# Four stores for the running products, an earlier fetch of block 1's decays, and five whole steps in a planned one-core kernel

## The chip, the core and the metric

The kernel runs on one core of one Trainium2 chip. The metric is the device time of one execution in microseconds (us), taken as the median of several runs. Engines are named as the profile names them: PE (TensorE; PEld is its weight load), DVE (VectorE), ACT (ScalarE), POOL (GpSimd) and SP (SyncE, whose queue SPq issues nearly all transfers here).

## The reference

Three layers follow one another. The first is a chunked linear recurrence over 4 batches, 8 heads and 768 positions; the other two are feed-forward layers on its output, each 256 to 2048 to 256.

```python
# recurrence, one chunk at a time (a is the decay, cum its running log sum)
L = np.exp(cum[:, :, :, None] - cum[:, :, None, :]) * causal
y_intra = np.einsum('bhij,bhjd->bhid', CB * L, xc)
y_inter = np.einsum('bhin,bhnd->bhid', Cc, state) * np.exp(cum)[:, :, :, None]
state = decay_full * state + np.sum(Bx, axis=2)
# layer 1 and layer 2, x is 3072 x 256
g = np.maximum(h, 0.0) + np.log1p(np.exp(-np.abs(h)))          # h = x @ w_in
g = np.where(h >= 1, h, np.where(h <= -1, 0.0, (h + 1) ** 2 / 4))
out = g @ w_out
```

## The kernel before

The sequence is cut into six blocks of 128 positions (`NC`), each for four batches, so there are 24 units `u` (block `u // 4`, batch `u % 4`). Block 0 makes its decay matrix on PE and ACT. Blocks 1 to 5 work on half blocks of 64: the clipped decays are stored once to a DRAM buffer `clip_z` (job `store`), then for each pair of units `rows` fetches them back, spread over 64 partitions (L1080, two transfers for a pair, one for each half), and `decay` turns them into the decay matrix by one scan on DVE (L1110). The running products of the decays are made by job `runs` (one scan on DVE at L1054), stored to the DRAM buffer `clip_p` by `store_runs` (L1059, one transfer for each of the blocks 1 to 5) and fetched for a block by `dec` (L1087), spread over the 16 state columns. `cd` (L1130, DVE) multiplies the unit's C by them, `carry` and `ready` use them for the state.

The two feed-forward layers are 192 steps `s`: a step takes one block's tokens and one of 16 slices of the hidden width (the first four steps take half a block's tokens and two slices). `up(s)` is the product with the input weights, `g(s)` the activation on ACT, `down(s)` the product with the output weights, accumulated in two PSUM banks of the block. To keep float32 accuracy, a number is split into a high and a low part (fp32r), and a product takes three matmuls (high by high, low by high, high by low; L1314 to L1316 for `up`, L1450 for `down`). The first `WHOLE` steps make their `down` otherwise: the activation is written in float32 straight into a `gh` buffer and the matmul runs on unsplit float32 operands (L1438). A step that isn't whole has two jobs more: `g_hi` (rounds the activation, L722, ACT or DVE) and `g_lo` (the remainder, L1424, DVE, or POOL for steps below 16), and its output weights must have been split (`w_hi` at L722, `split_w` at L955 on DVE or POOL). Until step 15, PE has two PSUM banks for `up`, so it can be two steps ahead of the activation. Weights arrive as 64-bit numbers and are made into float32 by `w0` to `w3` (L781 to L817) on ACT and DVE.

Nothing of the order is written by hand: `program` lists all jobs with an engine or a choice of engines, a cost, the jobs that they need and the buffers that they take, and `Jobs.order` simulates the engines in Python when the kernel is built and emits the jobs in the order in which that simulation started them. On each engine, SP's queue among them, instructions then run in this fixed order, so one that waits holds up all behind it. Constants steer the plan: `BIAS` is added to an engine's finish where there is a choice, `RATE` is the assumed rate of the transfers in bytes per ns, `RUSH` moves single jobs' due times (positive: sooner), `STAND_BY` lets a more urgent job go first, `CHUNK`, `SPACE` and `SHIFT` give the steps by which later blocks are due, `LAG_1` the due time of some `down` jobs. `BIAS_2` would apply to a `split_w` of the second layer on POOL; these have no such choice. In the first 26 us the emitter also puts fillers (bf16 matmuls on zeros, L1531) where the plan has PE idle.

Of the kernel before, what the change touches and what calls it, by code (L numbers as in the profile page):

```python
# [16 lines left out]
HALF = 64  # L17
# [10 lines left out]
class Jobs:  # L28
# [18 lines left out]
    def order(self, slots, begin):  # L47
# [33 lines left out]
        locked, shared = [], None  # L81
# [19 lines left out]
        for _ in range(len(jobs)):  # L101
# [25 lines left out]
            if engine == POOL:  # L127

                begun = start + 60
                for a, b in locked:  # L130
                    if a < begun + cost and b > begun:
                        begun = b
                shared = [name, begun, begun + cost]
                cost += begun - start
            elif engine == DVE and kind in LOCKED:
                if shared and start < shared[2] and start + cost > shared[1]:
                    if start <= shared[1]:
                        late = start + cost - shared[1]
                        shared[1] += late
                        shared[2] += late  # L140
# [11 lines left out]
            if engine == SP:  # L152
                pipe = max(pipe, end) + size / RATE
                end = pipe + BEHIND * (start < 5000.0 and size > 2e5)
            done = self.done[name] = end
# [84 lines left out]
def program():  # L240
# [34 lines left out]
    add("runs", DVE, 1500, needs=["clip", ("columns", 1)] + RUNS)  # L275
    for c in range(1, NC):
        add(("store_runs", c), SP, 600, needs=["runs"], size=16e3)
        add(("dec", c), SP, 400, needs=[("store_runs", i) for i in range(1, NC if c == 2 else 2)], takes=["dec"], size=262e3)
    for u in range(NU):
# [12 lines left out]
        else:  # L292
            if b % 2:
                add(("rows", u), SP, 1100, needs=["store"], takes=["lp"], size=524e3)
# [229 lines left out]
WHOLE = 8  # L524
# [19 lines left out]
BIAS = {DVE: 400, POOL: 500}  # L544
# [3 lines left out]
STAND_BY = 400  # L548
FAR = 10000.0
CHUNK = 9  # L550
BIAS_2 = 9000
RATE = 330.0
# [4 lines left out]
SHIFT = 2  # L557
LAG = 1500
LAG_1 = 9000
# [9 lines left out]
    ("decay", 2, 1): -8000, ("decay", 5): -16000, ("load_w", 1, "i", 2): -16000, ("w3", 0, "o", 4): 8000,  # L569
# [8 lines left out]
def tile_kernel(ctx: ExitStack, tc: tile.TileContext, a0, al, bc, ub, w_in, w_out, w2_in, w2_out, out):  # L578
# [132 lines left out]
    clip_z = dram.tile([NU, 2, H * HALF], F32, name="clip_z")  # L711
# [5 lines left out]
    clip_p = dram.tile([NC, H, NB * 2, HALF], F32, name="clip_p")  # L717
# [319 lines left out]
    def store(engine, *step):  # L1037
# [7 lines left out]
        else:  # L1045
            nc.sync.dma_start(clip_z.rearrange("u s (h i) -> (u s) h i", h=H), z_t)
# [9 lines left out]
    @job  # L1056
    def store_runs(engine, c):
        n = NB * 2
        nc.sync.dma_start(clip_p[c].rearrange("h r i -> r h i"), tiles["clip"][c * n:(c + 1) * n])  # L1059
# [16 lines left out]
    def rows(engine, u):  # L1076

        t = flat(buf(*got["rows", u][0])).rearrange("p (u f) -> p u f", u=2)
        for s in range(2):
            nc.sync.dma_start(  # L1080
                t[s * HALF:(s + 1) * HALF], clip_z[u - 1:u + 1, s].unsqueeze(0).to_broadcast([HALF, 2, H * HALF])
            )

    @job
    def dec(engine, c):
        src = clip_p[c].rearrange("h r i -> h (r i)")
# [498 lines left out]
```

## Time and profile before

| What | us |
|---|---|
| median of 3 runs | 557.3 (556.88 to 559.26) |
| the profiled execution, its own time | 557.88 |
| its span, first to last instruction | 556.2 |
| PE busy | 546.8 |
| DVE busy | 435.7 |
| ACT busy | 391.7 |
| POOL busy | 39.2 |

The span leaves out about 1.7 us ahead of the first and behind the last instruction. Busy time of PE counts fillers, and the ends of matmuls are modelled, so a busy PE is no proof of useful work. The granted clock of PE was 1.00 through the span.

### The profile page before, as it was taken

To read this page: it belongs to the slowest core of one execution; us is meant where nothing else is said; L and a number is where in the kernel's file an instruction comes from. 1 tells how busy PE (TensorE), PEld (TensorE's weight loads), DVE (VectorE), ACT (ScalarE), POOL (GpSimd) and SP (SyncE) were. 2 spreads that over 40 slices of the span, in tenths; PEclk is the share of its full clock that TensorE was granted. 3 is DMA by queue.
4 is the path that set the end of the run, shared out by engine and by line. 5 is a ranking of instruction groups with operands and counts; after the bars stand their busy time and mean duration, and the time that the engine had idled before them with its cause. 6 is when DMAs were issued, how large, how long until landed. Compare 5 with 4: busy or idle time off the path is not lost.

```text
span 556.2 us, 10449 instructions
## 1 busy us (share of the span) xinstructions
PE 546.8 (98%) x3994; PEld 442.3 (80%) x3994; DVE 435.7 (78%) x813; ACT 391.7 (70%) x720; POOL 39.2 (7%) x45
## 2 busy tenths in 40 slices
PE   9898999999999999999999999999999999999997
PEld 4765878878888888888888788888888888888885
DVE  6987999888865989876777898989886665876663
ACT  7968646645455666766566989786987875888773
POOL 3112220000000100001300000021310000000000
PEclk9999999999999999999999999999999999999999
DMA  8985467576242500276436314514100001100002
GB/s 280 392 220 178 138 194 210 165 235 183 93 165 75 180 1 1 96 258 205 143 113 214 128 59 152 171 56 130 62 1 0 1 1 38 39 0 1 1 1 76
DMA packets 34679, 64.73 MB, mean 116 GB/s; under 512 B 3684, under 2 KB 8164, under 8 KB 34628
## 3 DMA queue, kind: packets, MB, share of 16 engines
q1 hardware_dynamic: 34484, 63.93, 35.3%
q8 instruction: 31, 0.51, 0.4%
q14 instruction: 20, 0.16, 0.1%
q10 hardware_dynamic: 144, 0.13, 0.1%
HBM read 47.61 MB, written 16.43 MB: 115 GB/s over the span
## 4 chain that ended last, share of the span: by engine, by line
PE 87%; DMA 8%; DVE 2%; ACT 1%; SPq 1%; issue 1%; DVEq 0%; ACTq 0%
PE acc L1450 44%; PE h L1321 5%; PE h L1323 5%; PE h L1322 5%; PE z L1321 4%; PE z L1323 4%; PE z L1322 4%; PE h L1314 3%; PE h L1315 3%; PE h L1316 3%; DMA raw<-in_w_out_dram 2%; DMA ld<-clip_z 2%; DMA dec<-clip_p 2%; PE y L1223 1%; DMA st<-in_w_out_dram 1%; DMA u<-in_ub_dram 1%
## 5 line engine op out<-in xcount | busy, mean ns | idle before, releaser
L1424 DVE TENSOR_TENSOR gl<-g,gh 128x512 fp32r<-128x512 f32 x181 | 127.6, 709 | 55.1 <-PE acc L1450 31.0
L1450 PE MATMUL acc<-gh,woh 128*128 128x512 f32 x368 | 144.3, 392 | 0.0
L1450 PE MATMUL acc<-gh,wol 128*128 128x512 f32 x368 | 143.3, 389 | 0.0
L722 ACT CAST gh<-g 128x512 fp32r<-128x512 f32 x172 | 106.8, 621 | 26.4 <-PE acc L1450 14.2
L1450 PE MATMUL acc<-gl,woh 128*128 128x512 f32 x368 | 113.6, 389 | 0.0
L1450 PEld LDWEIGHTS acc<-gh,woh 128*128 128x128 f32 x368 | 69.1, 188 | 15.2 <-issue 0.5
L1450 PEld LDWEIGHTS acc<-gl,woh 128*128 128x128 f32 x368 | 69.1, 188 | 14.4
L1450 PEld LDWEIGHTS acc<-gh,wol 128*128 128x128 f32 x368 | 69.1, 188 | 14.1
L1409 ACT ACTIVATE g<-h 128x512 f32<-128x512 f32 x61 | 36.4, 597 | 51.7 <-PE h L1316 36.6
L1401 ACT ACTIVATE t<-t 128x512 f32<-128x512 f32 x96 | 60.9, 634 | 1.9
L1314 PE MATMUL h<-xh,wih 128*128 128x512 f32 (+1 forms) x114 | 46.0, 403 | 0.5 <-ACT wih L722 0.5
L1315 PE MATMUL h<-xh,wil 128*128 128x512 f32 (+1 forms) x114 | 42.9, 376 | 0.7 <-DVE wil L955 0.7
L1316 PE MATMUL h<-xl,wih 128*128 128x512 f32 (+1 forms) x114 | 42.9, 376 | 0.0
L1110 DVE TENSOR_TENSOR_SCAN ld<-ld,eye_t 128x512 f32<-128x512 f32 x20 | 25.1, 1289 | 4.0 <-DMA ld<-clip_z 2.7
L1394 ACT ACTIVATE t<-h 128x512 f32<-128x512 f32 x37 | 22.1, 598 | 7.8 <-PE h L1323 6.7
L1314 PEld LDWEIGHTS h<-xh,wih 128*128 128x128 f32 x114 | 21.4, 188 | 6.2 <-issue 1.1
L1413 DVE TENSOR_TENSOR g<-h,t 128x512 f32<-128x512 f32 x37 | 25.3, 685 | 1.1 <-ACT t L1401 0.3
L1394 ACT ACTIVATE t<-z 128x512 f32<-128x512 f32 x35 | 21.0, 599 | 7.1 <-DVE g L1413 3.9
L1315 PEld LDWEIGHTS h<-xh,wil 128*128 128x128 f32 x114 | 21.5, 188 | 5.6 <-DVE wil L955 1.0
L1413 DVE TENSOR_TENSOR g<-z,t 128x512 f32<-128x512 f32 x35 | 24.0, 686 | 1.5 <-ACT t L1401 0.5
L1316 PEld LDWEIGHTS h<-xl,wih 128*128 128x128 f32 x114 | 21.4, 188 | 4.0
L1409 ACT ACTIVATE g<-z 128x512 f32<-128x512 f32 x19 | 11.4, 598 | 17.4 <-PE z L1316 8.8
(320 smaller groups left out, 1008.0 us busy)
## 6 DMA issues: line engine op xcount, KB each, us to landing
st<-in_w_in_dram SPq DMA_DIRECT2D x15, 512.0 KB, 5.9
st<-in_w_out_dram SPq DMA_DIRECT2D x15, 512.0 KB, 6.7
u<-in_ub_dram SPq DMA_DIRECT2D x24, 256.0 KB, 6.2
ld<-clip_z SPq DMA_DIRECT2D x20, 256.0 KB, 6.0
bc<-in_bc_dram SPq DMA_DIRECT2D x12, 384.0 KB, 6.5
pre_i<-st_plain SPq DMA_DIRECT2D x15, 256.0 KB, 2.0
pre_s<-st_plain SPq DMA_DIRECT2D x14, 192.0 KB, 5.5
pre_o<-st_plain SPq DMA_DIRECT2D x10, 256.0 KB, 3.7
```

The costliest lines, as they stand in the source:

```text
L722: nc.scalar.copy(out, in_)
L1314: nc.tensor.matmul(o, wh, xh[c][:, k, t0:t0 + n], start=(k == 0), stop=False)
L1315: nc.tensor.matmul(o, wl, xh[c][:, k, t0:t0 + n], start=False, stop=False)
L1316: nc.tensor.matmul(o, wh, xl[c][:, k, t0:t0 + n], start=False, stop=(k == 1))
L1321: nc.tensor.matmul(bank, wh, bh, start=start, stop=False, skip_group_check=True)
L1322: nc.tensor.matmul(bank, wl, bh, start=False, stop=False, skip_group_check=True)
L1323: nc.tensor.matmul(bank, wh, bl, start=False, stop=True, skip_group_check=True)
L1401: nc.scalar.activation(out=t, in_=t, func=AF.Square, scale=0.5 / SAT, bias=0.5)
L1409: nc.scalar.activation(out=g, in_=ph, func=AF.Softplus)
L1413: nc.vector.tensor_tensor(out=g, in0=ph, in1=t, op=ALU.max)
L1424: engines[engine].tensor_tensor(out=mine("g_lo", s)[0], in0=mine("g", s)[0], in1=mine("g_hi", s)[0].bitcast(F32), op=ALU.subtract)
L1450: nc.tensor.matmul(acc_t(s, e), w, g[:, j * n:(j + 1) * n], start=(begins(e, j) and g is gh and i == 0), stop=(fc + j == NFC - 1 and g is ...
```

## The change

Five things are changed together.

1. `store_runs` is two jobs of two transfers each in place of five of one. Job 1 stores block 1 (one transfer for each half of a block), job 2 stores blocks 2 to 5. `dec(1)` needs job 1, all later `dec` need job 2. Before, `dec(1)` needed the first store, `dec(2)` all five, and later ones the first.
2. The DRAM buffers are laid out anew: `clip_z` by half first (a pair's `rows` transfer then reads one run of 4 KB where it read two of 2 KB), `clip_p` by head first. The host array `al` is transposed to match.
3. `WHOLE` is 5 in place of 8, so steps 5, 6 and 7 become split steps.
4. The planner's model: SP is given at most eight transfers in flight, `rows` and `dec` are charged more bytes, and the lock that POOL and DVE share is modelled more simply.
5. The planner's constants.

```diff
             if engine == POOL:
-                begun = start + 60
-                for a, b in locked:
-                    if a < begun + cost and b > begun:
-                        begun = b
-                shared = [name, begun, begun + cost]
+                begun = max([b for a, b in locked if a < start + 60 < b], default=start + 60)
+                shared = [name, begun, begun + cost, False]
...
+                flight += [end + 1500] * TRANSFERS.get(name if isinstance(name, str) else name[0], 1)
+                if len(flight) >= 8:
+                    clock[SP] = max(clock[SP], flight[-8])
...
+    for c in range(1, 3):
+        add(("store_runs", c), SP, 700, needs=["runs"], size=16e3 * (c * c))
     for c in range(1, NC):
-        add(("store_runs", c), SP, 600, needs=["runs"], size=16e3)
-        add(("dec", c), SP, 400, needs=[("store_runs", i) for i in range(1, NC if c == 2 else 2)], takes=["dec"], size=262e3)
+        add(("dec", c), SP, 400, needs=[("store_runs", min(c, 2))], takes=["dec"], size=262e3 * 1.5)
...
-                add(("rows", u), SP, 1100, needs=["store"], takes=["lp"], size=524e3)
+                add(("rows", u), SP, 1100, needs=["store"], takes=["lp"], size=524e3 * 1.6)
...
-WHOLE = 8
+WHOLE = 5
-BIAS = {DVE: 400, POOL: 500}
+BIAS = {DVE: 600, POOL: 1500}
-STAND_BY = 400
+STAND_BY = 300
-CHUNK = 9
-BIAS_2 = 9000
-RATE = 330.0
+CHUNK = 10
+BIAS_2 = 500
+RATE = 385.0
+TRANSFERS = {"rows": 2, "store_runs": 2, "split_w": 2, "put_w": 2, "put_s": 2, "get_s": 2}
-SHIFT = 2
+SHIFT = 1
-LAG_1 = 9000
+LAG_1 = 12000
 RUSH = {
-    ("decay", 2, 1): -8000, ("decay", 5): -16000, ("load_w", 1, "i", 2): -16000, ("w3", 0, "o", 4): 8000,
+    ("down", 31): -4000, ("sources", 9): -4000, ("w2", 0, "i", 5): 4000,
 }
...
-    clip_z = dram.tile([NU, 2, H * HALF], F32, name="clip_z")
+    clip_z = dram.tile([2, NU, H * HALF], F32, name="clip_z")
-    clip_p = dram.tile([NC, H, NB * 2, HALF], F32, name="clip_p")
+    clip_p = dram.tile([H, NU, 2, HALF], F32, name="clip_p")
...
     def store_runs(engine, c):
-        n = NB * 2
-        nc.sync.dma_start(clip_p[c].rearrange("h r i -> r h i"), tiles["clip"][c * n:(c + 1) * n])
+        a, b = ((NB, 2 * NB), (2 * NB, NU))[c - 1]
+        for s in range(2):
+            nc.sync.dma_start(clip_p[:, a:b, s].rearrange("h u i -> u h i"), tiles["clip"][s * NU + a:s * NU + b])
...
-                t[s * HALF:(s + 1) * HALF], clip_z[u - 1:u + 1, s].unsqueeze(0).to_broadcast([HALF, 2, H * HALF])
+                t[s * HALF:(s + 1) * HALF], clip_z[s, u - 1:u + 1].unsqueeze(0).to_broadcast([HALF, 2, H * HALF])
...
-        src = clip_p[c].rearrange("h r i -> h (r i)")
+        src = clip_p[:, c * NB:c * NB + NB].rearrange("h u s i -> h (u s i)")
```

## Rows read from the trace of the kernel before

**Rows 1.** The page: busy us of each engine, share of the span, instructions.

```profile
PE 546.8 (98%) x3994; PEld 442.3 (80%) x3994; DVE 435.7 (78%) x813; ACT 391.7 (70%) x720; POOL 39.2 (7%) x45
```

**Rows 2.** Waits of PE, whole span: us in total, times, longest.

```profile
PE acc L1438 <- ACT gh L1409: 2.1, 2, 1.5
...
PE h L1315 <- DVE wil L955: 0.7, 1, 0.7
PE h L1314 <- ACT wih L722: 0.5, 1, 0.5
PE z L1321 <- ACT h L1349: 0.2, 1, 0.2
```

**Rows 3.** Windows: stretch, busy us (instructions) of each engine, PE clock, DMA share, GB/s.

```profile
30.00:40.00 10.00, 10.00 (x39) 6.96 (x38) 9.66 (x17) 6.19 (x10) 0.00 (x0) 1.00 0.77 202
40.00:50.00 10.00, 8.27 (x27) 4.62 (x26) 5.30 (x13) 6.60 (x12) 0.00 (x0) 1.00 0.67 198
...
500.00:556.20 56.20, 52.12 (x230) 42.83 (x229) 33.16 (x51) 38.62 (x68) 0.00 (x0) 1.00 0.05 20
```

**Rows 4.** Timeline of PE, 19 to 80 us: start, us, instruction [idle before].

```profile
19.59 1.99 PE L1438 MATMUL acc<-gh,w 128*128 128x256 f32 x8 [1.51 <-ACT gh L1409]
...
35.00 0.80 PE L1314 MATMUL h<-xh,wih 128*128 128x512 f32 x1
...
38.11 0.80 PE L1314 MATMUL h<-xh,wih 128*128 128x512 f32 x1
...
43.72 1.98 PE L1438 MATMUL acc<-gh,w 128*128 128x512 f32 x4 [0.55 <-ACT gh L1409]
...
47.63 0.50 PE L1314 MATMUL h<-xh,wih 128*128 128x512 f32 x1 [0.53 <-ACT wih L722]
48.78 0.50 PE L1315 MATMUL h<-xh,wil 128*128 128x512 f32 x1 [0.66 <-DVE wil L955]
...
79.34 0.80 PE L1223 MATMUL y<-ld,u 64*32 64x64 f32 x60 [0.82 <-DVE ld L1166]
```

**Rows 5.** The chain in order of time, two split steps after another.

```profile
110.07 1.36 PE acc L1450 x6
112.79 1.36 PE acc L1450 x6
```

**Rows 6.** Timeline of DVE, 26 to 46 us.

```profile
26.61 1.68 DVE L817 SCALAR_TENSOR_TENSOR w<-st,w 128x512 uint32<-128x512 uint32 x1
...
40.04 0.68 DVE L955 TENSOR_TENSOR wol<-w,woh 128x512 fp32r<-128x512 f32 x1
45.42 0.90 DVE L1130 TENSOR_TENSOR u<-u,dec 128x128 f32<-128x128 f32 x4 [4.70 <-DMA dec<-clip_p]
```

**Rows 7.** Timeline of SP's queue, 23 to 35 us: start, us from first to last issue.

```profile
23.30 3.60 SPq L1080 DMA_DIRECT2D ld<-clip_z  x4
27.04 6.60 SPq L1059 DMA_DIRECT2D clip_p<-more  x5
34.25 0.41 SPq L769 DMA_DIRECT2D st<-in_w_in_dram  x1
```

**Rows 8.** The chain from 19 to 62 us: two transfers, issue to landing.

```profile
26.32 9.42 DMA ld<-clip_z
...
36.23 9.16 DMA dec<-clip_p
```

**Rows 9.** Waits of SP's queue, 20 to 50 us.

```profile
SPq L769 <- DVE w L817: 10.3, 2, 7.8
```

**Rows 10.** The page's groups: us busy, mean ns of one.

```profile
L1424 DVE TENSOR_TENSOR gl<-g,gh 128x512 fp32r<-128x512 f32 x181 | 127.6, 709 | 55.1 <-PE acc L1450 31.0
...
L722 ACT CAST gh<-g 128x512 fp32r<-128x512 f32 x172 | 106.8, 621 | 26.4 <-PE acc L1450 14.2
```

**Rows 11.** Timeline of POOL at 26 us: two products' low parts.

```profile
26.44 2.99 POOL L955 TENSOR_TENSOR wol<-w,woh 128x512 fp32r<-128x512 f32 x2 [10.89 <-ACT woh L722]
```

**Rows 12.** The page's transfers: KB each, median us from issue to landing.

```profile
pre_i<-st_plain SPq DMA_DIRECT2D x15, 256.0 KB, 2.0
```

More of the change, by code (lines that the diff above doesn't have):

```diff
@@ L80, in order @@
         held = {}
-        locked, shared = [], None
+        locked, shared, flight = [], None, []
         self.start, self.end, self.done = {}, {}, {}
@@ L136, in order @@
                 if shared and start < shared[2] and start + cost > shared[1]:
-                    if start <= shared[1]:
+                    if start <= shared[1] and not shared[3]:
                         late = start + cost - shared[1]
-                        shared[1] += late
-                        shared[2] += late
+                        shared[1:] = shared[1] + late, shared[2] + late, True
                         clock[POOL] = self.done[shared[0]] = shared[2]
@@ L1045, in store @@
         else:
-            nc.sync.dma_start(clip_z.rearrange("u s (h i) -> (u s) h i", h=H), z_t)
+            nc.sync.dma_start(clip_z.rearrange("s u (h i) -> (s u) h i", h=H), z_t)
     @job
@@ L1551 @@
     c6 = C.reshape(NB, H, NC, Q, N)
-    al = np.ascontiguousarray(a.reshape(NB, H, NC, 2, HALF).transpose(2, 0, 3, 1, 4)).reshape(NC * NB * 2, H * HALF)
+    al = np.ascontiguousarray(a.reshape(NB, H, NC, 2, HALF).transpose(3, 2, 0, 1, 4)).reshape(NC * NB * 2, H * HALF)
     a0 = np.ascontiguousarray(a6[:, :, 0]).reshape(NB * H, Q)
```

## The prediction

> **What bounds the kernel now.** I read the page first: PE is busy for 546.8 of 556.2 us, DVE for 435.7, the others for less [rows 1]. So the time is PE's work plus the few microseconds in which PE stood, and the next view is the list of PE's waits [rows 2]. Once PE has begun, it gives 4.3 us in six waits over the whole span; placed in the timeline, all but the 0.2 us of the wait for L1349 lie before 80 us [rows 2, 4]. The reader is to see that behind that point nothing is to be won but work taken off PE, and that a new order there can only lose. The tail of 4.1 us, where the last stretch has PE busy for 52.12 of 56.20 [rows 3], is the last copies and stores, which the change leaves alone.
>
> What is left ahead of 80 us: 1.51 us before 19.59 (the larger of the two waits at L1438), 0.55 before 43.72, 0.53 and 0.66 before 47.63 and 48.78, and 0.82 before 79.34 (block 2's products with its decay matrix) [rows 4]. To see why, I followed DVE back from the two waits at 48 us. DVE finished a split at 40.7 and then stood 4.70 us until block 1's running products landed (`cd`, L1130) [rows 6]; the weights of step 8, which PE wanted at 47.1, were queued behind it on DVE. The stretch from 40 to 50 us shows it from outside: DVE is busy for 5.30 of 10, PE for 8.27 [rows 3]. The running products were late because of SP's queue: four row transfers from 23.3, five stores from 27.0 to 33.6, weight loads from 34.25, and only then the fetch at 36.23, which took 9.16 us to land [rows 7, 8].
>
> **What the change takes and costs, part by part.** *Three steps less on float32.* A whole step runs six split matmuls and its float32 `down`: the periods at 35.00 and 38.11 are 3.11 us apart [rows 4]. A split step is twelve matmuls in two groups, 2.72 us (110.07 to 112.79) [rows 5]. Three steps give 3 x (3.11 - 2.72) = 1.17 us of PE work. This is the surest term, since PE is full from 19.6 to 43 us.
>
> *What these three steps ask for instead.* Each needs a rounding (0.62 us, ACT) and a remainder (0.71 us on DVE) [rows 10], or a remainder on POOL at 1.5 us, half of the 2.99 us that two like products took there [rows 11]: 3 x 0.71 = 2.1 us of DVE, and the low parts of two pieces of the output weights, which the old order made at leisure, are due some 10 us sooner. I cost this at nothing, because the 4.70 us hole in DVE's queue [rows 6] covers the 2.1 us if the decays come in time. If that cover is gone, up to 2.1 us land on PE. Making them on POOL has a price too: the L817 at 26.61 took 1.68 us while POOL was at its products from 26.44, where another product of that size takes DVE 0.68, so a POOL product can cost DVE about 1.0 us [rows 6, 11]. The higher bias against POOL should make that rarer and give DVE 0.7 us for each product moved back, so the two nearly cancel.
>
> *The decays fetched sooner.* Four transfers go out in place of five, and block 1's fetch waits for the first two of them, which are half a block's products each. With the stores no longer all ahead of it, the fetch can go out from about 27 to 32 instead of 36.23; an estimate from the same queue is that it lands 4 to 9 us sooner. DVE reached the wait at 40.7, so 4.70 us sooner is enough: the hole closes, and the 0.53 and 0.66 us at PE [rows 4] with it: 1.19 us. What is late next on that path is the weights themselves: SP had waited up to 7.8 us for a staging buffer that DVE's last weight operation frees (L769 behind L817) [rows 9], and that wait sits behind the same hole, so I expect it to shrink, not to take over.
>
> *The wait at 43.7.* PE stood 0.55 us for the activation of step 7, written late because ACT stood for a weight load in its queue [rows 4]. Step 7's `down` is split after the change, so it follows later and PE takes the next `up` first. I take all of the 0.55; the bounds are 0 and 0.55.
>
> *Rows by halves.* Each `rows` transfer reads runs of 4 KB, not two of 2 KB; one of them took 9.42 us [rows 8]. At best the scans of block 1 start some us sooner. They end on no PE wait here, so I cost it at nothing, with block 2's 0.82 us [rows 4] as the upper bound of what it can give.
>
> *The new constants and the model of SP.* They reorder everything. Behind 80 us PE stood 0.2 us, so a gain there is excluded but a loss isn't; in the first 20 us PE waits for ACT's first activation, and ACT's choice of work there may move either way by one operation, 0.6 us [rows 10]. I take zero, bounds -1.5 (the first wait at L1438 gone) and +2.6 (new waits as large as all those that the old order has from 40 to 80 us: 0.55 + 0.53 + 0.66 + 0.82 [rows 4]).
>
> *A rule weighed against the rows.* On the first two stores, the nearest row for a small transfer to DRAM is 2.0 us to landing (256 KB, later in an idle stretch), and the farthest 9.42 us, for the `rows` transfer that stood in the queue at the same time [rows 8, 12]. The Trainium skill, DMA: Bandwidth & Descriptors, "Anatomy of one DMA — SWDGE (gpsimd) path", puts the fixed cost at about 2.0 us and says that a semaphore wait happens on the issuing sequencer before dispatch; the idle row agrees with the figure, and no row here shows a store's landing under load; by its 2.0 us the fetch would go out about 2 us behind the first store and the sum would be the same 554.4. By the row of 9.42 us SP would stand up to 9 us with the weights behind it, and that is the slower rival below.
>
> **The sum.** On the profiled execution's own 557.88: 1.17 + 1.19 + 0.55 = 2.91, which gives 554.97. That execution lies 0.6 above the median of 557.3, so on the median it is 554.4.
>
> **The rivals.** *More than that.* With SP's queue modelled by what it can hold, the 0.82 us of block 2 and half of the first 1.51 us go as well: another 1.6 makes 552.8. For it speaks that both waits are for work that other engines could have done sooner; against, that the first of them waits for ACT's first activation, to which the change does nothing that the code shows.
>
> *The gain is spent on the new work.* The three split `down` steps need 2.1 us of DVE and two pieces of weights sooner, in the stretch from 30 to 45 us where DVE would now be full. Then a wait of 1 to 3 us for a low part takes the place of those removed: 555.4 to 557.4, inside 0.5% of before. For it: DVE is nearly full in the old order already (9.66 of 10 in the slice before the hole) [rows 3].
>
> *The change doesn't do what it says.* The fetch still lands behind 40 us, since the transfers ahead of it are the bound and not the stores; only the 1.17 us stay: 556.1.
>
> *Slower.* SP's queue is in order. If the fetch of block 1 stands for the landing of its stores while the stores queue behind a megabyte of rows, the landing takes up to 9.42 us [rows 8], and the weight loads behind it (from 34.25 in the old order [rows 7]) go out by as much later. PE needs these weights from 47.1, and waited 1.19 us for them already; with 7 us more it would end at 557.3 - 1.2 + 7 = 563.1. It turns the sign once the delay on PE is more than the 2.9 us gained, and passes 0.5% at 5.7 us. Against it: the rows go out 3.6 us ahead in the old order and most of their landing time is over when the stores end.
>
> **How the numbers follow.** The forecast of 554.4 has 45 in 100, with 553.4 to 555.6 as its own range; more gain 20, the gain spent on new work 20, no effect but the 1.17 us 5, slower 10. A measurement of this kernel tells about 0.5%, 2.8 us, from no change, so faster means below 554.5. Of the forecast's 45, a little over half fall below that, so with the 20 of more gain it is 46 in 100. Same is the rest of the forecast, the spent gain and the lone 1.17 us: 43. Slower is the last rival and the bad end of spent gain: 11. The range that holds 8 in 10 runs from 552.3, the lower end of more gain, to 557.4, the upper end of spent gain.
>
> **What would show each step.** Right: four L1059 issues, the first two ahead of the first L1087; the fetch landing before 40 us; no wait of L1130 for it over 1 us; L1438 at five steps, 9 us or less of PE; L1314 and L1315 without waits around 48 us; PE's waits between 20 and 80 us at about 0.8 us in all. Wrong: PE waiting at L1450 for `gl` or `wol` between 35 and 55 us (the gain was spent), SP standing at L1087 with L769 behind it (the slower rival), waits of PE behind 80 us (the new order), or a first wait at L1438 above 1.5 us. The prediction falls if PE's work has not become about 1.2 us shorter, or if new waits ahead of 80 us exceed 1 us in sum.

## The result and the profile after

The changed kernel takes 564.0 us (563.56 to 564.25, four runs) against 557.3 (556.88 to 559.26) beside it: ratio 1.0126, 95% interval 1.0109 to 1.0144. It is slower by 1.3%, some 7 us. A second set of runs of the same kernel gave 564.6 (561.87 to 565.86), ratio 1.0134 (1.0100 to 1.0168). The forecast of 554.4 and its range are both missed, on the side that had 11 in 100. The profiled execution took 563.56 with a span of 561.8.

The first line of the page answers to [rows 1]:

```profile
PE 549.1 (98%) x3998; PEld 445.1 (79%) x3998; DVE 441.8 (79%) x804; ACT 401.7 (71%) x738; POOL 36.7 (7%) x42
```

PE is no less the bound than before, and DVE and ACT do more. PE's waits over the whole span answer to [rows 2] (L1533 belongs to the fillers, L1483 lies at the very start):

```profile
PE acc L1440 <- ACT gh L1411: 3.0, 1, 3.0
PE h L1323 <- POOL xh_later L725: 1.6, 1, 1.6
PE h L1483 <- DVE idle L1481: 1.1, 1, 1.1
PE y L1225 <- DVE ld L1168: 1.0, 3, 0.5
PE h L1533 <- ACT ld L1114: 0.6, 1, 0.6
PE acc L1203 <- issue: 0.6, 1, 0.6
PE z L1323 <- DVE z L1366: 0.5, 2, 0.3
```

The code has grown by two lines, so L1440 is L1438 of before, L1225 is L1223, and so on. The two waits for split weights (L1314, L1315) and the second one at L1438 are gone, as forecast. But the first wait at the `down` has doubled from 1.51 to 3.0 us, and there is a new 1.6 at L1323, in the second layer. In the timeline of PE they stand here, beside [rows 4]:

```profile
20.49 3.78 PE L1440 MATMUL acc<-gh,w 128*128 128x256 f32 x8 [3.01 <-ACT gh L1411]
...
48.27 0.80 PE L1225 MATMUL y<-ld,u 64*32 64x64 f32 x60 [0.53 <-DVE ld L1168]
...
50.27 0.30 PE L1203 MATMUL acc<-u,bt 64*32 64x64 f32 x3 [0.56 <-issue]
...
72.87 0.63 PE L1225 MATMUL y<-ld,u 64*32 64x64 f32 x32 [0.24 <-DVE ld L1168]
...
399.67 0.47 PE L1323 MATMUL h<-eye_later,wih 128*128 128x512 f32 x1 [1.62 <-POOL xh_later L725]
```

Two things besides the waits are to be seen. The first group of `down` took 3.78 us where it took 1.99. And block 1's products with its decay matrix (L1225) come at 48.27 us; before, they came at 57.03: the new order does block 1 nine microseconds sooner. The windows (columns as in [rows 3]) show what both mean:

```profile
20.00:26.00 6.00, 5.51 (x17) 4.53 (x18) 5.48 (x10) 4.24 (x10) 0.00 (x0) 0.50 1.05 304
...
30.00:40.00 10.00, 10.00 (x45) 8.14 (x44) 10.00 (x10) 9.29 (x19) 2.58 (x2) 1.00 0.80 247
40.00:50.00 10.00, 9.18 (x216) 6.78 (x215) 10.00 (x21) 7.96 (x14) 3.30 (x3) 1.00 0.59 202
500.00:561.80 61.80, 57.69 (x255) 47.45 (x253) 36.66 (x56) 43.52 (x77) 0.00 (x0) 1.00 0.05 18
```

Behind the wait of 3.01 us the granted clock is 0.50, the lower level of 1.2 GHz, for six microseconds. And DVE, which stood for 4.70 us between 40 and 50 before, is busy for 10.00 of 10 in both stretches: there is no slack left on it there. The tail (the last window: 61.80 less 57.69 is 4.1 us) is as it was.

**Where the 5.6 us lie.** The last matmul starts at 557.30, before at 551.74: 5.6 us later. Taken apart between the starts of successive matmuls, PE's idle time behind its first instruction is 7.48 us against 4.23, so 3.25 more, and the rest, 2.32, is matmuls that took longer. The lower clock is more than all of that: from 20.49 on, the eight matmuls of `down` and the nine of `up` behind them took 5.9 us from start to start, and seventeen of the same kind took 2.9 before. So all other work of PE has become some 0.7 us shorter (an estimate from these starts). The idle time goes, before to after: 12 to 20 us 1.51 to 3.62; 20 to 82 us 2.55 to 1.57; behind 82 us 0.17 to 2.30. So in this execution the stretch that the prediction was about did gain, and the loss stands on both sides of it.

Ahead of it: ACT's timeline, where it makes the first activation.

```profile
15.18 0.68 ACT L784 ACTIVATE w<-st 128x512 f32<-128x512 f32 x1 [0.68 <-DMA st<-in_w_in_dram]
16.53 0.70 ACT L784 ACTIVATE w<-st 128x512 f32<-128x512 f32 x1 [0.67 <-DMA st<-in_w_out_dram]
...
18.55 1.28 ACT L1410 ACT_TABLE_LOAD   x1
19.84 0.60 ACT L1411 ACTIVATE gh<-h 128x512 f32<-128x512 f32 x1
```

The plan now counts on 385 bytes per ns, and it put two `w0` jobs at places where their weights had not landed; ACT stood 1.35 us for them with other work queued behind, and the activation came at 19.84 instead of 18.94.

SP's queue, against [rows 7, 8]:

```profile
27.84 1.36 SPq L1061 DMA_DIRECT2D clip_p<-more  x2
...
33.55 1.39 SPq L1061 DMA_DIRECT2D clip_p<-more  x2
35.27 0.66 SPq L1089 DMA_DIRECT2D dec<-clip_p  x1
...
39.45 0.61 SPq L1089 DMA_DIRECT2D dec<-clip_p  x1
...
SPq L1089 <- DMA clip_p<-more: 0.5, 1, 0.5
```

Block 1's fetch goes out at 35.27, one microsecond sooner than before (36.23), not at 27 to 32. SP itself stands only 0.5 us for a store at a fetch (the last line, from its waits), because other loads stand between. But the fetch lands sooner by more than that: the last update of its semaphore in the trace is at 39.5, 4.2 us behind the issue, where it took 9.16 before and landed at 45.4 [rows 8]. DVE doesn't wait for it:

```profile
30.49 1.77 DVE L818 SCALAR_TENSOR_TENSOR w<-st,w 128x512 uint32<-128x512 uint32 x1
...
36.76 1.70 DVE L818 SCALAR_TENSOR_TENSOR w<-st,w 128x512 uint32<-128x512 uint32 x1
...
40.70 0.48 DVE L1120 TENSOR_TENSOR bt<-u,ld 128x128 f32<-128x128 f32 x2
...
43.57 2.38 DVE L1120 TENSOR_TENSOR bt<-u,ld 128x128 f32<-128x128 f32 x2
...
49.67 1.35 DVE L1132 TENSOR_TENSOR u<-u,dec 128x128 f32<-128x128 f32 x1
```

`cd` (L1132) stands at 49.67 in DVE's order, 4.25 us later than before, behind the scans and splits that were pulled ahead of it. So two things close the hole: the decays would have been there at 40.7, when DVE came to the wait before, and the new order fills that time with other work. The row at 43.57 shows one price of it: two `bt` products took 2.38 us, where two took 0.48 at 40.70, while POOL was at its own products:

```profile
43.21 1.30 POOL L956 TENSOR_TENSOR wil<-w,wih 128x512 fp32r<-128x512 f32 x1 [5.30 <-ACT wih L723]
44.47 1.34 POOL L956 TENSOR_TENSOR wol<-w,woh 128x512 fp32r<-128x512 f32 x1
```

The two rows of L818 show the same: 1.77 and 1.70 us beside POOL products at 30.44 and 36.60, where one takes 0.68 alone.

### The profile page after: what moved, and what is told of

Read it like the earlier page. It is cut to its first block, busy times and chain, and to the rows that moved or that the text cites. A ratio compares the mean times of both kernels' runs of the same rounds, so it can differ in the third digit from the quotient of the medians.

```text
span 561.8 us, 10489 instructions
## 1 busy us (share of the span) xinstructions
PE 549.1 (98%) x3998; PEld 445.1 (79%) x3998; DVE 441.8 (79%) x804; ACT 401.7 (71%) x738; POOL 36.7 (7%) x42
## 4 chain that ended last, share of the span: by engine, by line
PE 81%; DVE 10%; DMA 3%; issue 2%; ACT 2%; SPq 2%; POOL 0%; DVEq 0%; ACTq 0%; POOLq 0%
PE acc L1452 40%; PE h L1323 4%; PE h L1325 4%; PE h L1324 4%; PE z L1323 4%; PE z L1325 4%; PE z L1324 4%; PE h L1316 3%; PE h L1318 3%; PE h L1317 3%; DVE gl L1426 2%; DMA st<-in_w_out_dram 2%; PE y L1225 1%; DMA u<-in_ub_dram 1%; PE y L1257 1%
## 5 line engine op out<-in xcount | busy, mean ns | idle before, releaser
L1426 DVE TENSOR_TENSOR gl<-g,gh 128x512 fp32r<-128x512 f32 x183 | 129.5, 708 | 71.6 <-PE acc L1452 46.7
L1452 PE MATMUL acc<-gh,woh 128*128 128x512 f32 x374 | 147.0, 393 | 0.0
L1452 PE MATMUL acc<-gh,wol 128*128 128x512 f32 x374 | 145.7, 390 | 0.0
L723 ACT CAST gh<-g 128x512 fp32r<-128x512 f32 x176 | 109.1, 621 | 26.7 <-PE acc L1452 18.2
L1452 PE MATMUL acc<-gl,woh 128*128 128x512 f32 x374 | 115.4, 389 | 0.0
L1411 ACT ACTIVATE g<-h 128x512 f32<-128x512 f32 x65 | 38.8, 597 | 41.3 <-PE h L1318 30.7
L1316 PE MATMUL h<-xh,wih 128*128 128x512 f32 (+1 forms) x116 | 45.4, 391 | 0.0
```

The lines of the kernel that those rows point to most:

```text
L723: nc.scalar.copy(out, in_)
L1316: nc.tensor.matmul(o, wh, xh[c][:, k, t0:t0 + n], start=(k == 0), stop=False)
L1411: nc.scalar.activation(out=g, in_=ph, func=AF.Softplus)
L1426: engines[engine].tensor_tensor(out=mine("g_lo", s)[0], in0=mine("g", s)[0], in1=mine("g_hi", s)[0].bitcast(F32), op=ALU.subtract)
L1452: nc.tensor.matmul(acc_t(s, e), w, g[:, j * n:(j + 1) * n], start=(begins(e, j) and g is gh and i == 0), stop=(fc + j == NFC - 1 and g is ...
```

## The experiments

All ratios are to the kernel before, on the same chip. "After" is the changed kernel. Of each version one execution was profiled, so a wait that is compared between versions below is that of a single execution.

| run | what it is | us | ratio (95%) |
|---|---|---|---|
| c1_after_again | after, unchanged | 564.55 | 1.0134 (1.0100 to 1.0168) |
| e1_act_order | after, ACT's first weights in the order of before | 565.13 | 1.0137 (1.0107 to 1.0167) |
| e2_fillers | after, 13 fillers ahead of the first `down` | 565.32 | 1.0129 (1.0084 to 1.0174) |
| e5_before_act_order | before, with ACT's late order | 558.04 | 1.0008 (0.9990 to 1.0026) |
| e6_lock | after, e1 and two products from POOL to DVE | 563.57 | 1.0125 (1.0096 to 1.0153) |
| e7_before_rows_sooner | before, block 1's rows sooner | 559.73 | 1.0060 (1.0034 to 1.0086) |
| e8_before_stores | before, four stores, fetch behind the first two | 557.50 | 1.0019 (1.0000 to 1.0038) |
| e9_rows_later | after, block 1's rows later | 565.11 | 1.0146 (1.0132 to 1.0160) |
| e3_late_t | after, late work of DVE moved back | 566.89 | 1.0168 (1.0135 to 1.0200) |
| e10_t_spread | after, the same work spread | 563.16 | 1.0107 (1.0090 to 1.0124) |
| e11_after_whole8 | after, eight whole steps | 569.98 | 1.0227 (1.0208 to 1.0246) |
| e12_all | after, e6, e9 and e10 together | 567.03 | 1.0174 (1.0160 to 1.0188) |
| f1_after_lag | after, `LAG_1` 9000 | 568.68 | 1.0198 (1.0174 to 1.0222) |
| f2_before_lag | before, `LAG_1` 12000 | 559.01 | 1.0030 (1.0014 to 1.0046) |
| f3_after_code | changed code, all constants of before | 558.74 | 1.0022 (1.0009 to 1.0034) |
| f4_before_code | code of before, all changed constants | 565.69 | 1.0147 (1.0124 to 1.0169) |
| g2_after_code_whole5 | f3 with five whole steps | 558.61 | 1.0019 (0.9999 to 1.0039) |
| g1_after_rate | after, `RATE` 330 | 562.21 | 1.0079 (1.0051 to 1.0107) |

### One place at a time: the start

The first theory was that the late activation and the fall of the clock behind it make the loss. `ahead(a, b)` and `behind(b, a...)` move a job in the finished order, and `on_dve(a, b)` further down gives a job of POOL to DVE, behind `b`.

```diff
+    ahead(("w1", 0, "o", 0), ("w0", 0, "i", 1))      # e1: after
+    ahead(("w1", 0, "i", 1), ("w0", 0, "o", 1))
...
+            if name == ("down", 0):                  # e2: after
+                for i in range(13):
+                    nc.tensor.matmul(                #     on zeros
...
+    ahead(("w0", 0, "i", 1), ("w1", 0, "o", 0))      # e5: before
+    ahead(("w0", 0, "o", 1), ("w1", 0, "o", 0))
```

Expected of e1:

> The changed kernel with two ACT operations moved: two shifts of weights (w1 of the first output and second input piece) go ahead of the scalings (w0) for which ACT stood 0.68 and 0.67 us until a transfer landed. Theory (the start costs 3.5 to 3.8 us: the first activation came 0.9 us later, PE stood 3.0 us and its granted clock fell to 0.50 for 7 us): ACT's first activation ends about 1.3 us sooner, PE's wait shrinks to about 1.6 us, the clock stays at 1.00, and the time falls by 3.5 to 4 us to 560. Rival (only the lateness counts, the clock falls either way): 1.3 us, to 562.7. Rival (the loss is elsewhere, behind 200 us): no change.

Expected of e2:

> The changed kernel with 13 fillers (matmuls on zeros, 0.22 us each) put on PE ahead of the first down product, where PE stood 3.0 us; nothing else moves. Theory (the fall of the clock is the larger part): the down product still begins at about 20.5 us, the clock stays at 1.00 and 2.5 to 2.7 us are saved, to 561.4. Rival (the clock falls for another reason, or costs nothing): no change, 564.

Expected of e5:

> The kernel before with the change's order of these operations on ACT alone: the scalings of the second input and output piece ahead of two shifts. Theory: ACT stands for the landings, the first activation comes about 1 us later, PE stands 2.5 us or more, the clock falls to 0.50, and the time grows by 3 to 4 us, to 560.8. Rival (the lateness alone): 1 us, to 558.3. Rival (the start is not where the change loses): no change, 557.3.

Expected of the control:

> The changed kernel again, unchanged, beside the next three on one chip, since the runs so far gave its edits times of 563 to 567 us with other waits than its own first profile shows. Theory (the start varies little from chip to chip): 564, with the wait of 3.0 us at the first down product and 0.5 us at 48 us. Rival (the transfers at the start vary between chips, and so do the waits behind them): 565 to 567, with a wait of about 2 us at 49 us, so that the edits before did win something.

The control is to be read first. In its profiled execution (565.43 us, against 563.56 of the first one) the unchanged kernel has other waits:

```profile
PE acc L1440 <- ACT gh L1411: 4.0, 1, 4.0
PE y L1225 <- DVE ld L1168: 3.0, 4, 2.3
```

The first wait is 4.03 us at 21.25, and 2.29 stand at 49.84 before block 1's products, where the first profile has 0.53 at 48.27. So one trace's waits differ from the next by as much as the edits were to win.

Both edits did their local work: the first wait fell to 1.7 us in e1, and the granted clock stayed at 1.00 at that place in both. Neither shortened the kernel. The clock fell later instead, to 0.50 for 3.4 us from 49.5 in e1 and from 49.3 in e2, at a wait of 2.28 and 2.26 us; the window of e1 shows it as 0.85 on the average:

```profile
50.00:60.00 10.00, 10.00 (x227) 8.09 (x211) 10.00 (x22) 6.63 (x15) 1.58 (x1) 0.85 0.51 150
```

In e1 ACT also stood further on for a weight that comes late anyway:

```profile
32.49 0.76 ACT L802 ACTIVATE t<-st,low_bias 128x512 uint32<-128x512 uint32 x1 [4.06 <-DMA st<-in_w_out_dram]
```

and PE waited 0.92 us at 26.96, and the 2.28 at 49.09 for block 1's decay matrix. In e2 the waits came at 35.97, 46.03 and 49.73 (0.71, 0.65, 2.26). The wait at 49 us can't be put down to the edits, since the control has it too. The converse is clearer: e5 gives the kernel before the late start. Its first activation comes at 20.85 us instead of 18.94, PE waits 2.51 us at 19.43, the clock is 0.50 from 20 to 22, and all of it costs nothing that can be told from zero; the waits at 43 to 49 us of [rows 4] are gone in its trace instead. So in the kernel before a later start is taken out of the waits that follow it ahead of 50 us. The start by itself isn't the loss.

### One place at a time: block 1's rows and stores, and the lock

The second theory: with block 1 pulled ahead, its row transfers crowd the weights, and its DVE work stands beside POOL's.

```diff
+    ahead(("rows", 5), ("load_w", 0, "o", 3))               # e7: before
+    ahead(("rows", 7), ("load_w", 0, "i", 4))
...
+    ahead(("dec", 1), ("store_runs", 2))                    # e8: before, with the changed
+    # clip_z, clip_p and store_runs of two transfers         #     layouts and four stores
...
+    behind(("load_w", 0, "o", 4), ("rows", 5), ("rows", 7)) # e9: after
+    behind(("w2", 0, "o", 3), ("decay", 4), ("decay", 5))
...
+    on_dve(("split_w", 0, "i", 4), ("sources", 7))          # e6: after, with the
+    on_dve(("split_w", 0, "o", 1), ("weigh", 7, 1))         #     two lines of e1
```

Expected of e7:

> The kernel before with one thing of the change: the rows of block 1 asked for sooner, each pair's two transfers ahead of a weight load (third output piece, fourth input piece) on SP's queue instead of behind four more loads. Theory (rows use up the transfer engines' time, weights land later, ACT and DVE stand for them): new waits of PE of 1 to 3 us ahead of 50 us, 558.5 to 560.5. Rival, as I forecast it (rows sooner cost nothing and end on no wait of PE): 557.3, or up to 0.8 us less.

Expected of e8:

> The kernel before with one thing of the change: the two DRAM buffers laid out anew, four stores in place of five, and the fetch of block 1's decays directly behind the first two; all else in the old order. Theory of the forecast: the fetch lands 4 to 9 us sooner, DVE's 4.70 us hole and PE's two waits at 48 us go, 1.2 us are saved, 556.1. Rival (SP stands for the landing of its stores, with weight loads behind it): PE's waits at 44 to 49 us grow, 558 to 560. Rival (the transfers ahead are the bound): the fetch lands less than 2 us sooner, no change.

Expected of e9:

> The changed kernel with the rows of block 1 put back behind two weight loads, two unit loads and the fifth output piece's load on SP's queue, about where the old order has them, and with two of DVE's scans that use them put two operations later. Theory (the rows sent ahead of weights are the main loss before 60 us: they took 2.9 us from the old kernel too, where ACT stood for a weight): ACT's waits for weights at 25 to 33 us go, PE's waits between 20 and 50 us fall by 2 us or more, 561.5 to 562.5 against 564.5. Rival (block 1's scans come later by as much, and PE waits for block 1 at 49 us as before): 564 to 565.

Expected of e6:

> The changed kernel with the two ACT operations moved as in the first experiment, and with two products of weights' low parts (fourth input piece, first output piece) made on DVE in 0.66 us each, where POOL made them at 43.2 to 45.8 us in 1.3 us each beside DVE's two products for block 1, which took 2.4 to 2.7 us there where two of them take 0.5 elsewhere. Theory (POOL's products hold up DVE, DVE's products of block 1 are what PE waits for at 49 us): the wait of 2.3 us at 49 us falls to 1 us or less, the clock stays at 1.00 from 50 to 57 us, and the time is 2.5 to 4 us below that of the first experiment: 561 to 562.5. Rival (DVE is simply full there): the wait stays within 0.5 us of 2.3, no gain.

e7 is the one moved place that costs the kernel before something clear: 0.6%, with a new wait of 3.25 us at 37.45, where ACT stood for a weight behind the rows. But e9, its converse in the changed kernel, wins nothing: DVE then stands 5.0 us for the rows, and PE waits 1.97 at 41.84 and 1.37 at 51.83 in place of what it lost before. e6 has 0.86 at 47 us for the wait of 2.28 in e1 (2.29 in the control on its chip), its `bt` products take 0.48 us each pair, and its clock stays at 1.00, as its theory had it; but its ratio is 0.0012 below e1's, 0.7 us, well inside the intervals, and not 2.5 to 4.

e8 shows the stores by themselves, SP's queue and one line of its waits:

```profile
27.59 2.04 SPq L1069 DMA_DIRECT2D clip_p<-more  x2
35.28 0.64 SPq L1097 DMA_DIRECT2D dec<-clip_p  x1
...
SPq L1097 <- DMA clip_p<-more: 6.7, 2, 5.6
```

The fetch is the next instruction on SP, and it goes out 5.65 us behind the end of the stores' issue (27.59 + 2.04 = 29.63): SP stands for their landing. So in this order the fetch can't leave at 27 to 32; the soonest of all runs is 32.00, in e12, whose stores went out at 21.94. Yet here too it lands sooner, at 39.1 by its semaphore, 6.3 us ahead of before; DVE doesn't stand for it, and of PE's waits from 40 to 50 us 0.36 are left of 1.73. That much is as the forecast's theory had it. But the 1.2 us don't reach the end: 557.5 against 556.9 beside it. The loads queued behind the fetch left at 37.0 to 38.0, and DVE now stands 1.69 and 1.15 us for weights that ACT has to make first. In the profiled execution the first wait is 1.97 us with a lower clock behind it, at a place that the edit doesn't touch.

### Behind 220 us

The third theory: the new wait of 1.62 us at 399.67 comes from late work of DVE and POOL (the `t` jobs of the second layer's third group, made beside each other) and can be taken back by moving it.

```diff
+    behind(("add2", 34), ("t_sum", 3, 0))                   # e10: after; six lines like this
+    behind(("add2", 35), ("t_sum", 3, 2))                   # e3 puts them in four places
+    behind(("keep", 36), ("t_hi", 3, 0), ("t_hi", 3, 2))
...
-LAG_1 = 12000
+LAG_1 = 9000                                                # f1: after; f2: before, the other way
```

Expected of e3:

> The changed kernel with the sums and splits of the last group of blocks (t_sum, t_hi, t_lo of group 3, due at 426 us in the plan, run from 389 to 401 us) moved two to five groups of four steps later. Theory (the 1.6 us for which PE stood at 399 us comes from these operations, on DVE ahead of the additions that PE needed and on POOL beside them): that wait goes and 1.4 to 1.8 us are saved, to 562.4. Rival (the wait is for something else, or moves along with them): no change, 564.

Expected of e10:

> The changed kernel with the sums and splits of the last group of blocks spread over four later quads, ACT's parts behind its copies for PE (in the third experiment they stood ahead of them, and new waits of 0.95 and 0.97 us took the place of the old one). Theory (the 1.6 us at 399 us come from these operations alone): that wait goes, no other comes, 562.9 against 564.5. Rival (the queues behind 380 us are full enough that any place costs as much): 564 to 565.

Expected of f1:

> The changed kernel with LAG_1 at 9000 again; its order is the same up to 225 us. If the later due time of some down jobs makes the new waits of PE behind 220 us (about 3.4 us of lag), the time falls to 560 to 561.5 and PE's waits behind 220 us add up to under 0.5 us. If they come from the choice of engines or from work that is already late at 220 us, the time stays at 563 to 565.

Expected of f2:

> The kernel before with LAG_1 at 12000 and nothing else; its order is the same up to 230 us. If the later due time makes the late waits, it costs 2 to 3.5 us: 559 to 561. If not, 557 to 558.

The wait went in both e3 and e10, and new ones came: 0.95 and 0.97 at 421 and 431 us in e3, 0.95 at 417 in e10. e10 has the lowest time of those that keep the changed constants, 563.16: some 1 to 1.5 us better than after, with overlapping intervals, and still 1.1% behind. `LAG_1` isn't what costs the changed kernel its time: set back, it makes that kernel worse by some 4 us (PE waits 3.57 us at 316.9 and 1.34 at 311.7), so the theory gave f1 the wrong sign. Put into the kernel before, it costs 0.3%.

### Everything together, and the whole steps

e12 has the lines of e1, e6, e9 and e10 at once; e11 is one constant.

```diff
-WHOLE = 5                     # e11: after and this
+WHOLE = 8
```

Expected of e12:

> The changed kernel with four of the edits together: the two ACT operations of the first experiment, the two products on DVE in place of POOL, the rows later, the last group's sums and splits spread. Theory (start, rows, POOL's lock and the late group are the whole loss, and 1.2 us of PE work are really saved): waits of PE at 2 to 3 us in all behind the first microsecond, 556 to 558, level with the kernel before. Rival (the losses hide one another, so that less than half adds up): 560 to 562.

Expected of e11:

> The changed kernel with eight whole steps instead of five; the planner makes a new order from 24 us on, the same ahead of it. Theory of the forecast (three whole steps cost PE 1.17 us and PE is the bound): 1.2 us more, 565.7. Rival (transfers, DVE and POOL set the pace from 20 to 50 us, so that five whole steps save nothing there and ask DVE for three remainders and PE for split weights sooner): 562 to 564.5, with shorter waits of PE ahead of 55 us.

e12, with all these edits in one, is slower than after itself: 1.0174. Its trace has eight waits of PE above 0.5 us, at other places again (among them 1.86 at 50.55 and 1.46 at 75.17). e11 was replanned from 24 us on and lost 3.28 us at 76.77 and 1.75 at 236.7. It shows how much a replanned order can cost, and not what a whole step is worth. Both runs lie outside all that was expected of them.

### Code against constants

So no single place is the cause. The next four runs therefore split the change along another line. Line by line in the source, one part is code (stores, layouts, the planner's model), the other the constants.

```diff
-WHOLE = 5                     # f3: changed code, this and the
+WHOLE = 8                     #     other eight constants as before
...
-LAG_1 = 9000                  # f4: old code, all nine
+LAG_1 = 12000                 #     constants as changed
...
-WHOLE = 8                     # g2: f3 and this
+WHOLE = 5
...
-RATE = 385.0                  # g1: after and this
+RATE = 330.0
```

Expected of f3:

> The changed kernel's code (four stores, layouts, planner's model) with all constants of the kernel before, eight whole steps among them. If the code, that is the fetch behind its stores and the new model, costs the time, 561 or more with PE's waits ahead of 80 us above 5 us. If the constants cost it, 556 to 559.

Expected of f4:

> The code of the kernel before (five stores, old layouts, old model of the queue) with all constants of the changed kernel, five whole steps among them. If the constants cost the time, 562 or more. If the code costs it, 556 to 559. If each costs about half, 559 to 561 here and in the kernel with the changed code alone.

Expected of g2:

> The changed code with all constants of the kernel before, but five whole steps in place of eight. If the work taken off PE (1.17 us) reaches the end, 557.0 to 558.2, that is 0.5 to 1.7 us below the same kernel with eight whole steps (558.7). If the three split steps' roundings, remainders and weights are not hidden, 559 to 563, with new waits of PE between 30 and 60 us for gl, wol or what stands behind them on DVE.

Expected of g1:

> The changed kernel with RATE alone at 330 again (all other constants and the code as changed). If the higher assumed rate, which asks for the first weights and for block 1's rows sooner than the transfers move, costs most of the loss, the time falls to 556.5 to 559, with the first wait at the down below 1.6 us and PE's waits ahead of 82 us under 3 us. If the loss lies in the other constants (bias, shift, five whole steps), 562 to 566.

Here the cause comes apart. The constants in the old code cost 1.47%, as much as the whole change; the new code with the old constants costs 0.2%. Taken as steps from before to after: the code 0.2%; five whole steps nothing that shows (1.0022 to 1.0019, with some 1.3 us of noise either way); all other constants but the rate 0.6% (to 1.0079); the rate 0.5% (to 1.0126, in the control 1.0134). The intervals of g2, g1 and after (0.9999 to 1.0039, 1.0051 to 1.0107, 1.0109 to 1.0144) lie apart, so the last two steps are clear of the noise, and each is some 3 us; only the control's wider interval (from 1.0100) reaches into g1's. They are steps between single orders, though. One constant turned in either direction moved the time by 0.3% up (f2), 0.7% up (f1), about 1% up (e11) or 0.5% down (g1). Whether 385 is a worse rate as such, or the new constants made an order that is worse because nothing else was tuned to it, these runs don't separate. f3, where the old constants make a new order too, speaks against the latter as the whole cause.

f3 is also the fair trial of the mechanism that the prediction was about. PE's waits:

```profile
PE acc L1452 <- DVE gl L1426: 1.2, 1, 1.2
PE y L1257 <- ACT sm L1295: 1.1, 1, 1.1
PE h L1483 <- DVE idle L1481: 1.1, 1, 1.1
PE acc L1440 <- ACT gh L1411: 0.9, 1, 0.9
PE h L1323 <- DVE h L1366: 0.9, 1, 0.9
```

Between 20 and 50 us PE doesn't wait at all (before: 1.73 us). DVE starts `cd` sooner than before and finds its decays there:

```profile
43.51 0.89 DVE L1132 TENSOR_TENSOR u<-u,dec 128x128 f32<-128x128 f32 x4
```

No wait stands in that row; it is 1.9 us sooner than the 45.42 of [rows 6], though the fetch left at 35.40 (it landed at 42.1). From 12 to 50 us the waits fall from 3.24 to 1.04 us. Then they come back: 1.11 at 61.5 (before: 0.82 at 79.34), 1.24 at 186.83 for a remainder that DVE makes late, 0.86 at 391.5; behind 50 us 3.27 against 0.99. What was gained ahead of 50 us, 2.2 us, is given back as 2.3 us behind it, in a stretch in which the order has changed too. DVE has no more slack here than in after, as its third pair of numbers shows (columns as in [rows 3]), and POOL is at work for 9.2 us beside it:

```profile
30.00:40.00 10.00, 10.00 (x38) 6.96 (x38) 10.00 (x11) 6.29 (x11) 6.07 (x4) 1.00 0.96 304
40.00:50.00 10.00, 10.00 (x39) 6.89 (x38) 9.56 (x18) 8.40 (x16) 3.13 (x3) 1.00 0.55 195
```

PE is busy for all of both stretches. So a full DVE from 30 to 50 us is not by itself what costs after its time.

g2's waits, next to f3's:

```profile
PE acc L1452 <- DVE gl L1426: 1.8, 2, 1.2
PE h L1323 <- DVE h L1366: 1.2, 1, 1.2
...
PE h L1317 <- DVE wil L956: 0.7, 1, 0.7
```

The three split steps do bring waits for `gl` and `wil` at 47 and 50 us (0.56 and 0.67), as the rival "spent on the new work" had it. PE's time between the starts of its matmuls, waits left out, is 546.1 us against f3's 546.5: 0.4 us less, not 1.17. Two profiles don't tell 0.4 from nothing: e7, with eight whole steps, has 545.7. A part of the saving is lost around the waits: the twelve matmuls of two `up` that take 2.72 us in f3 (from 47.42) take 3.16 in g2 (from 49.19), the wait among them left out.

f4's waits, in the line numbers of before:

```profile
PE acc L1438 <- ACT gh L1409: 4.1, 1, 4.1
PE y L1223 <- DVE ld L1166: 3.7, 4, 2.9
PE y L1255 <- ACT sm L1293: 2.3, 1, 2.3
```

With the old stores and the old model of the queue, the constants alone bring the late activation (4.1 us) and the waits for block 1's and 2's decay matrices (3.7). In this kernel they arise from the order, not from the transfers' new form.

g1's profiled execution was its slowest (563.47, its median 562.21), so its trace says little about the gain. Its first wait is 2.3 us, between 1.5 and 3.0, ACT stands 0.26 us for the weights where it stood 1.35, a wait of 1.26 at 399.6 is still there, and one of 1.86 stands at 50.06. By its own terms the run fell to the rival (562 to 566), at its edge. Which of the other constants (`BIAS`, `CHUNK` with `SHIFT`, `STAND_BY`, `RUSH`) costs the other half stays open: none was tried by itself. No version tried beats the kernel before.

## Why the prediction was wrong

*Which step failed.* "The new constants and the model of SP": the prediction said that they reorder everything, and then "I take zero, bounds -1.5 and +2.6". That term measures +8.3 us in the old code (565.69 less 557.36; the whole steps are in it); in the changed code the rate makes about 3 us of the loss and the other constants about 3. It was the largest term of the change and was put at nothing. The upper bound was the sum of the waits that the old order happens to have between 40 and 80 us, which says nothing of what another order can have: over all the runs here, PE's waits between 12 and 82 us went from 2.2 us (f3) to 10.7 (f4), and a single one up to 4.1. It also priced a wait at its own length: the first wait of after is 1.5 us longer than before, and the lower clock behind it took 3.0 us more.

*The decays fetched sooner.* The effect was right, the way to it only in part. The fetch lands sooner, by 5.9 us in after, 6.3 in e8 and 3.3 in f3, against the 4 to 9 forecast. But it goes out only 0.8 to 1 us sooner there (and later in g2, at 37.58), not at 27 to 32, since the landing of two small stores takes SP 5.65 us (e8). The gain is in the fetch's own time, 3.9 to 6.7 us for 9.16, of which the prediction said nothing; what makes it shorter is not shown. Of the second pair of stores, of 32 KB each, the traces tell one landing each: 4.8 to 5.2 us in after, f3 and g2, 3.4 in e8. The prediction weighed a rule of the Trainium skill, DMA: Bandwidth & Descriptors, "Anatomy of one DMA — SWDGE (gpsimd) path", with about 2 us of fixed cost. That section is on transfers that GpSimd issues, and its figure leaves the moving of the bytes out; these go by SP's queue, and under this load their landing took 3.4 us to over 5.6, so here the rows decide, not the figure. The rule's other half, that the wait stands on the issuing sequencer, is what e8 shows. The hole on DVE closed all the same, and in f3 the waits of 0.53, 0.66 and 0.55 us with it: 1.74 forecast, 1.73 measured from 20 to 50 us. The forecast was the sum of these waits, so the match says that all of them are gone, in one execution of each. The 0.55 went by another way than the one given: the prediction had it go because step 7 is split, and in f3 step 7 is whole. That part is luck.

*The slower rival.* SP did stand at the fetch with loads queued behind, for 5.65 us in e8; that by itself cost the kernel before 0.2%, not 1%. In after the planner put other loads between, and SP stands 0.5 us. The time came out on its side of zero, but by another mechanism.

*Three steps less on float32.* 1.17 us forecast, at most 0.4 measured on PE (g2 against f3), none that shows at the end: there are 1.2 us of new waits for the remainders and weights that these steps ask for. The range of the rival "spent on the new work", 1 to 3 us, covers that.

*Work costed at nothing.* The prediction named its cover, the hole of 4.70 us on DVE. The changed kernel fills that hole: DVE is at 10.00 of 10 from 30 to 50 us. The higher bias against POOL was to make its products rarer; from 26 to 50 us POOL begins five where it began two, and the price of about 1.0 us of DVE for each is borne out (1.77 and 1.70 us for 0.68 beside one, 2.38 for 0.48 beside two). With the cover gone, POOL's lock, late rows and late weights each end on PE in one run or another, and each edit that removes one meets another (e1, e2, e6, e9, e12). That this is how the constants make the loss is argued, not shown: in f3 DVE is as full and PE doesn't wait.

*Rows by halves, block 1 sooner.* Costed at nothing, with a gain as the bound. The row transfers land in a median of 5.7 us for 6.0 (the pages), so the longer runs alone give little. Asking for block 1's rows sooner costs the kernel before 0.6% by itself (e7). The prediction had noted that a new order behind 80 us "can only lose", and still put zero for it: waits of PE behind 82 us are 2.30 us after against 0.17, and 2.2 in f3.

What the runs don't settle: how much of after's loss belongs to the late stretch (e10 is 1 to 1.5 us lower, inside the intervals), which constants other than the rate make it, and through which waits.

## What to carry to other kernels

When a change touches the constants of a planner that lays out a whole kernel, those constants are the change: swap code and constants against each other first, since those two runs told more here than all edits of single places. Profile the unchanged kernel a second time before an edit of one wait is judged: here its first wait was 3.0 us in one execution and 4.0 in the other, and the wait at 49 us 0.5 and 2.3. A tuned order is a balance of queues in which PE's waits trade against each other, so a wait that a trace shows is worth only what the next queue behind it leaves, and the order that removes it must be priced for the stretches that it doesn't mean to touch. Removing one stall, or putting one in, says little of the end: e5 made the start 1.9 us later and lost nothing, e1 made it sooner and won nothing.

## What the runs showed of the hardware

Two products on DVE took 2.38 us while POOL ran two of its own, and 0.48 us alone. The Trainium skill, SBUF — State Buffer, "SBUF: two separate sides", says that GpSimd and a DVE operation that reads two inputs from SBUF, as these do, hold their shared port pair as an exclusive lock for a whole instruction; the trace agrees: 43.57 + 2.38 = 45.95 lies just behind POOL's end at 44.47 + 1.34 = 45.81.

Stores of 32 KB to DRAM took 3.4 to 5.2 us to land among the row transfers and weights, and the 2.0 us for 256 KB of [rows 12] were no guide to that. With the transfer engines fully busy (1.05) they moved 304 GB/s from 20 to 26 us, where rows and weights run together, against 391 from 19 to 20.

A wait of 3.01 us on PE at 20 us came with a granted clock of 0.50, 1.2 GHz, for the next six microseconds, in which the group of `down` took 3.78 us for 1.99; in e1 a wait of 1.7 us at the same place left the clock at 1.00. The length of a wait alone doesn't decide it: in e7 the clock stayed at 1.00 through the wait of 3.25 us at 37.45, and in e8 it fell to 0.50 behind one of 1.97 at 20.33; of the two waits at 49 us, 2.28 us in e1 and 2.29 in the control, only the first was followed by the lower clock.
